# One ring for inputs and attention outputs, per-unit clock figures, and ScalarE row spreads in a two-layer attention kernel

## Chip, core and metric

The kernel runs on one core of a Trainium2 chip. The metric is the device time of one execution in microseconds (us): the median of three runs, 1835.46 us, with the lowest at 1834.81 and the highest at 1835.81.

## What is computed

Two independent attention layers, A and B, each with an input x of 2048 x 1024, a projection `wqkv` (1024 x 3072), 32 heads of size 32, and an output projection `wo` (1024 x 1024), all in float32. Their outputs are set side by side.

```python
qkv = (x @ wqkv).reshape(B, S, 3, 32, 32)            # q, k, v of each head
# A: each position looks at itself and 7 earlier ones, two apart
idx  = pos[:, None] - (arange(8) * 2)[None, :]       # masked where idx < 0
# B: each position looks at the last 256
mask = (i - j >= 0) & (i - j < 256)
out  = softmax(q k^T * 32**-0.5, masked) @ v         # per head
y    = out.reshape(B, S, 1024) @ wo
concatenate([a, b], axis=-1)
```

## The kernel before

**Units.** The work is cut into eight units of 512 positions: four of layer B ("dense" units, 0 to 3), then four of layer A ("window" units, 4 to 7). Each unit has eight head groups s = 0 to 7 of four heads. For a group the kernel computes q and k (`qk_items`, matmul at L526); values come in three parts of four, two and two groups (`v_items`, L591); the output projection of a unit (`o_items`, L652) runs within the next unit. A float32 product is made of three matmuls on a high and a low part of each operand.

**Splits.** Weights and x arrive by DMA in raw tiles. `Stream.parts` makes the high part by a cast, on ScalarE (L203) or VectorE (L206), and the low part by a subtraction on VectorE (L209). Items are split in one order. x tiles come from a pool of 9, the outputs of attention (`finish`: high part by ScalarE, L838, low part by VectorE, L842) from another of 10.

**Dense heads.** The first pass multiplies keys and queries (L873); VectorE masks and finds the maximum (L878); ScalarE exponentiates in place and sums (L883). From maximum and logarithm of the sum comes one number a row, as high and low part (L901 to L904). A small matmul turns the numbers into rows (L912). The row spread writes them below the 96 rows of the queries, VectorE in four instructions, one for each head (L918); keys have ones there, so that the second pass (L956) gives logarithms of the weights at once. ScalarE exponentiates them (L963), GpSimd or VectorE zeroes what is masked (L942, L945), and L1003 multiplies with the values.

**Window heads.** Scores at L722, softmax on VectorE and ScalarE (L730 to L758), a transpose (L761), and a placement of its pieces by ScalarE, eight pairs of copies a head (L770, L773). L788 multiplies with the values.

**The order of the work.** Nothing is reordered on the chip. When the program is built, a planner with a clock of its own (class `Clock`) keeps the expected time at which each engine is free. In turn it takes, from four lists (row matmuls, second passes, first passes, projections), the entry that can start first, writes it out for TensorE, and charges prices such as these:

```python
if ck.ends("act", n / 1200 + 0.06, t0) <= ck.ends("dve", n / 1932 + 0.08, t0) + bias:
e = ck.use("dve", 0.61, ck.now)          # one row spread
```

An engine waits on semaphores for real inputs, so an entry that the planner set too early makes TensorE wait. `MASK_BIAS`, `KEYS_LATE`, `ROWS_LATE`, `SEAT_LATE`, `EDGE_LATE` and `BANK_LATE` are allowances in this clock. `ASK` says after which of an item's eight steps the next weights are split. `V_SLOTS` and `O_SLOTS` say after or before which group's q and k a value part or an output projection stands.

**Unit edges.** The last value part of a unit (16 projection steps) holds the split of the next unit's x, at its steps 1, 5, 9 and 13 (`XAT`). Since items are split in order, the first of these brings the second half of the value weights and the next unit's first q weights with it.

Of the kernel before, what the change touches and what calls it, by code (L numbers as in the profile page):

```python
# [32 lines left out]
V_SLOTS = {0:0,5:1,7:2}  # L33
O_SLOTS = {2: (0, 1), 3: (2, 3), 4: (4, 5), 5: (6, 7)}
V0_SLOTS = {1:0,3:1,7:2}
NX, NST, NN = 9, 1, 3
TAIL, XAT = 4, 1
# [3 lines left out]
BANK_LATE = 0.0  # L41
# [91 lines left out]
class Stream:  # L133
# [3 lines left out]
    def __init__(self, nc, ck, raws, wpool, xpool, items, more, light):  # L137

        self.nc, self.ck, self.raws, self.wpool, self.xpool, self.more = nc, ck, raws, wpool, xpool, more
        self.items = items  # L140
        self.raw, self.tiles, self.ready = {}, {}, {}
        self.loaded = self.split = 0
        self.light = light
        self.load_to(NRAW + len(more))
# [20 lines left out]
    def split_to(self, n):  # L165
        while not self.split:
# [3 lines left out]
            for h in range(2):  # L170
                c = slice(h * S, h * S + S)
                self.tiles[0].append(self.xpool.tile([P, 2, S], F32R, tag="x", name="x"))
                self.ready[0].append(self.parts(self.tiles[0][h], rx[:, c], tx[h], True))
                self.ready[1].append(self.parts(w[:, :, c], rw[:, c], tw[h], True))
# [3 lines left out]
        while self.split < min(n, len(self.items)):  # L178
# [3 lines left out]
            if self.items[i][0] != "w":  # L182
                self.tiles[i], self.ready[i] = [], []
                for h in range(2):
                    t = self.xpool.tile([P, 2, S], F32R, tag="x", name="x")
# [10 lines left out]

    def parts(self, t, raw, t0, side):
# [3 lines left out]
        bias = EARLY if side else LIGHT if self.split >= self.light else SIDE_W if n > S else SIDE_X  # L201
        if ck.ends("act", n / 1200 + 0.06, t0) <= ck.ends("dve", n / 1932 + 0.08, t0) + bias:
            nc.scalar.copy(t[:, 0, :], raw)  # L203
            r = ck.use("act", n / 1200 + 0.06, t0)
        else:
            nc.vector.tensor_copy(t[:, 0, :], raw)  # L206
            r = ck.use("dve", n / 1932 + 0.08, t0)
# [5 lines left out]
    def ahead(self, i, two):  # L213

        for n in range(i + 1, min(i + (3 if two else 2), len(self.items))):
            if self.items[n][0] == "x":
                break
            self.split_to(n + 1)
# [7 lines left out]
def kernel(ctx, tc, xs, wqk, wv, wo, outs, units):  # L226
# [11 lines left out]
    pickp = ctx.enter_context(tc.tile_pool(name="pickp", bufs=1))  # L238
    opool = ctx.enter_context(tc.tile_pool(name="opool", bufs=NO))
# [11 lines left out]

    plan = []
    for u in range(U):
        for s in range(NG):
            if u and s in O_SLOTS:
                plan += [("o", u - 1, n) for n in O_SLOTS[s]]
            plan.append(("qk", u, s))
            vs = V_SLOTS if u else V0_SLOTS
# [7 lines left out]
    def item(key, kind, ap):  # L266
        where[key] = len(items)
        items.append((kind, ap))

    def unit_x(u, *gs):  # L270
        for g in gs or range(4):
            item(("x", u, g), "x", xs[u][:, 2 * g:2 * g + 2, :])

# [5 lines left out]
    for p in plan:  # L279
# [3 lines left out]
        elif p[0] == "v":  # L283
            s0, n = VPARTS[p[2]]
# [6 lines left out]
        elif p[0] == "qk":  # L291
            for t in range(2):
                if p + (t,) not in where:
                    item(p + (t,), "w", wqk[ly, 2 * p[2] + t])
        else:
            if NG - 1 in V_SLOTS:
                item(("qk", p[1], 0, 0), "w", wqk[units[p[1]][0], 0])
                unit_x(p[1])
            else:
                unit_x(p[1], 0)  # L300
                item(("qk", p[1], 0, 0), "w", wqk[units[p[1]][0], 0])
                unit_x(p[1], 1, 2, 3)
# [3 lines left out]
                where[("qk",) + LIGHT_FROM + (0,)] if LIGHT_FROM[0] < U else len(items))  # L306
# [6 lines left out]
    def constants():  # L313
# [13 lines left out]
        pick = cst["pick"] = pickp.tile([32, 16], F32, name="pick")  # L327
        nc.gpsimd.memset(pick, 0.0)
        for row in (0, 16):
            nc.gpsimd.affine_select(pick, pick, pattern=[[-1, 16]], compare_op=ALU.not_equal, fill=1.0, base=-row,  # L330
                                    channel_multiplier=1)
# [14 lines left out]
        def ones():  # L346
            zero = cst["mask_d"][96:P, None, P:2 * P].to_broadcast([32, 24, P])
            for t in kst:
                nc.scalar.activation(t[96:P, :, :].rearrange("p j (a s) -> p (j a) s", s=P), zero, AF.Identity,
                                     bias=1.0, scale=1.0)  # L350
                ck.use("act", 2.7, ck.now)
# [4 lines left out]
    vbuf = [const.tile([P, 6, n * P], F32, name=f"vbuf{i}") for i, (_, n) in enumerate(VPARTS)]  # L356
    vpart = {s0 + i: (p, i * P) for p, (s0, n) in enumerate(VPARTS) for i in range(n)}
# [46 lines left out]
    def qk_items(u, s):  # L404
# [36 lines left out]
        def by_head(c0, c1, e):  # L441

            def go():
# [4 lines left out]
                if c0:  # L448
                    done["nat"][nat] = e2
                    done["stack"][u, s] = e2 + (EDGE_LATE if s == NG - 1 and u + 1 < U else SEAT_LATE)  # L450
# [7 lines left out]
        def evac(t, ps, bank):  # L458
# [7 lines left out]
            def low():  # L466
# [5 lines left out]
                def stack():  # L472
                    e2 = place(1, e)
                    if t == 1:
                        done["stack"][u, s] = max(e2, h2["hi"]) + KEYS_LATE
# [29 lines left out]
        for t in range(2):  # L505
# [15 lines left out]
            def run(k, t=t, h=h):  # L521
# [6 lines left out]
                if k == ASK:  # L528
                    st.ahead(where["qk", u, s, t], not dense and TWO)
# [22 lines left out]
    def v_items(u, part):  # L552
# [5 lines left out]
        s0, ng = VPARTS[part]  # L558
# [47 lines left out]
        def ahead(i):  # L606
            st.ahead(i - 1, TWO and not units[u][2] and not wide)

        def after(r, n, k, b):
            if n == len(rounds[r]) - 1 and k == kw - 1:  # L610
                per = 1 if wide else 2
                c = (4 * u + (2 * r + b if wide else 2 * b)) % 6
                t = copy_out(vbuf[part][:, c:c + per, :], h[b][0].rearrange("p (a f) -> p a f", a=per), h[b][1], rg)
# [15 lines left out]
    def o_items(u, n):  # L629
# [15 lines left out]
        def run(k):  # L645
# [8 lines left out]
            if k == ASK and (not last or n == 0 or n > 2):  # L654
                if last:
                    st.split_to(where["o", u, n] + (3 if n == 0 else 2))
                else:
                    st.ahead(where["o", u, n], TWO and u + 1 < U and not units[u + 1][2])
# [32 lines left out]
    def window(u, s):  # L691
# [5 lines left out]
        vp, vc = vpart[s]  # L697
        v = vbuf[vp]
# [53 lines left out]
        def total(e):  # L752
# [7 lines left out]
            for i in range(2):  # L760
                nc.vector.transpose(turned[i], band[buf][:, 768 * i:768 * i + 768])  # L761
                e = ck.use("dve", 1.02, ck.now)
                ck.defer(e - 0.1, lambda i=i, e=e: spread(i, e))

        def spread(half, e):
            pieces = turned[half].rearrange("p (j b t c) -> p j b t c", j=2, b=4, t=3)
            diag = wide[buf][:, 2 * half:2 * half + 2].rearrange("p j (b c) -> p j b c", b=4)
            for i in range(4):
                r, c = 32 * i, 32 * i + 8
                nc.scalar.copy(diag[r:r + 32, :, :, c:c + 32], pieces[r:r + 32, :, :, 1 + i % 2, :])  # L770
                ck.use("act", 0.34, e)
                n, c = ((i - 1) * 32, c) if i else (96, 0)
                nc.scalar.copy(diag[n:n + 32, :, :, c:c + 8], pieces[r:r + 32, :, :, i % 2, :8])  # L773
                t = ck.use("act", 0.21, e)
            if half:
                h["p"] = t

        def values_ready():
            if hg >= NO and ((hg - NO) // NG, NG - 1) not in done["out"]:
# [70 lines left out]
    def attention(u, s):  # L850
# [6 lines left out]
        vp, vc = vpart[s]  # L857
        v = vbuf[vp]
# [35 lines left out]
        def log_sum():  # L894
# [4 lines left out]
            def parts():  # L899
# [5 lines left out]
                e2 = ck.use("dve", 0.52, e, port=True)  # L905
                aux.append(Item(lambda: latest(rs.when(BANK_LATE), e2), lambda: rows(hl), 0.08))

            ck.defer(e, parts)

        def rows(hl):  # L910
# [3 lines left out]
            def spread():  # L914

                h["rows"] = []
                for j in range(4):
                    nc.vector.tensor_tensor(q[96:P, j, :].rearrange("p (b s) -> p b s", s=P),  # L918
                                            ps[0:32, None, 0:P].to_broadcast([32, 4, P]),
                                            cst["pick"][0:32, 4 * j:4 * j + 4, None].to_broadcast([32, 4, P]), op=ALU.mult)  # L920
                    e = ck.use("dve", 0.61, ck.now)
                    h["rows"].append(e + ROWS_LATE)
# [4 lines left out]
        for b in range(4):  # L927
            for j in range(4):
                one.append(Item(lambda: latest(rs.when(BANK_LATE), done["stack"].get((u, s))),
# [9 lines left out]
        def keep(w, mask, n, m, step, base, chan, r):  # L939
            dur_p, dur_d = m * n / 960 + 0.13, m * n / 960 + 0.07  # L940
            if ck.ends("pool", dur_p, r) <= ck.ends("dve", dur_d, r, port=True) + MASK_BIAS:
# [39 lines left out]
        def second_ready(ki, hp):  # L981
# [4 lines left out]
            return latest(rs.when(BANK_LATE), h["rows"] and h["rows"][hp * pack + pack - 1])  # L986

        def values_ready(ks):
            if ks[-1] == nk - 1 and hg >= NO and ((hg - NO) // NG, NG - 1) not in done["out"]:
# [27 lines left out]
        for i, ks in enumerate(lots):  # L1017
            for ki in ks:
                pack = kbs[ki][3]
                for hp in range(4 // pack):  # L1020
# [3 lines left out]
                            C3 + sum(kbs[k][2] / 592 for k in ks)))  # L1024
# [9 lines left out]
    xt[0], xready[0] = [], []  # L1034
    for p in plan:
# [111 lines left out]
```

## Time and profile before

| quantity | value |
|---|---|
| median of three runs | 1835.46 us |
| the profiled execution | 1834.72 us |
| its span | 1832.6 us |
| TensorE matmul busy | 1805.0 us |
| weight loads busy | 1468.2 us |
| VectorE / ScalarE / GpSimd busy | 1300.5 / 966.2 / 395.3 us |
| mean granted TensorE clock | 0.996 |

A row of the waits says which line on which engine stood still, who ended that, how long in total, how often, and the longest. A row of the timeline has start, length, engine, line, operation, tiles and count; in square brackets is the idle time before it. A row of stages has the stage, its length, the busy time and count of TensorE, weight loads, VectorE, ScalarE and GpSimd, the granted clock, the share of the DMA engines and GB/s.

### The profile page before, as it was taken

The numbers are of one execution on the slowest core, as the hardware profiler recorded it, in microseconds if no ns is written. First come the engines' busy times: TensorE is split into PE (matmuls) and PEld (weight loads), VectorE is DVE, ScalarE is ACT, GpSimd is POOL, SyncE is SP. The second block draws the span as 40 slices with busy tenths as digits, with TensorE's granted clock in tenths as the row PEclk, the third lists the DMA queues.
The fourth block names the chain that finished last, engine by engine and source line by source line (L and its number), as shares of the span: only waits on it lengthen the run. The fifth ranks groups of instructions, "written<-read, shape, count | busy, mean of one in ns | idle before, by whom it ended". The sixth has DMA issues, their size and how long they took to land.

```text
span 1832.6 us, 34542 instructions
## 1 busy us (share of the span) xinstructions
PE 1805.0 (98%) x12778; PEld 1468.2 (80%) x12778; DVE 1300.5 (71%) x2718; ACT 966.2 (53%) x2520; POOL 395.3 (22%) x920
## 2 busy tenths in 40 slices
PE   9999999999999999999999999999999999999999
PEld 7787787888778788788887688878887788778887
DVE  6677886768867679776687486776667667766773
ACT  5566566565655555656555364544445444534452
POOL 2322313232242324232223200110011100110000
PEclk9999999999999999999999999999999999999999
DMA  7445665545555556545444333343434443434332
GB/s 242 125 134 139 177 169 144 170 121 166 160 154 163 152 146 174 141 149 144 135 136 139 106 126 128 127 133 127 136 120 133 138 132 107 156 122 138 123 104 81
DMA packets 109128, 257.20 MB, mean 140 GB/s; under 512 B 14496, under 2 KB 29856, under 8 KB 108960
## 3 DMA queue, kind: packets, MB, share of 16 engines
q0 software_dynamic: 41760, 152.06, 26.7%
q1 hardware_dynamic: 56832, 83.00, 17.0%
q10 hardware_dynamic: 10368, 19.93, 2.9%
q8 instruction: 101, 1.65, 0.4%
q14 instruction: 67, 0.55, 0.1%
HBM read 164.63 MB, written 23.07 MB: 102 GB/s over the span
## 4 chain that ended last, share of the span: by engine, by line
PE 90%; ACT 5%; DVE 3%; issue 1%; DMA 1%; POOL 0%; ACTq 0%; POOLq 0%; DVEq 0%
PE g L526 36%; PE g L652 19%; PE g L591 16%; PE s L956 5%; PE s L873 5%; PE o L1003 5%; PE o L788 2%; ACT wide L770 2%; PE s L722 1%; ACT wide L773 1%; DVE band L758 1%; DVE sm L754 1%; DVE w L209 1%; DMA raw<-xs 1%; ACT s L883 0%
## 5 line engine op out<-in xcount | busy, mean ns | idle before, releaser
L526 PE MATMUL g<-x,w 128*128 128x512 f32 x3072 | 774.9, 395 | 3.7 <-DVE w L206 1.7
L526 PEld LDWEIGHTS g<-x,w 128*128 128x128 f32 x3072 | 565.9, 189 | 118.0 <-issue 5.8
L591 PE MATMUL g<-w,x 128*128 128x256 f32 (+1 forms) x2304 | 389.3, 320 | 2.0 <-DVE w L209 2.0
L209 DVE TENSOR_TENSOR w<-raw,w 128x512 fp32r<-128x512 f32 x516 | 337.5, 696 | 34.7 <-ACT w L203 27.7
L591 PEld LDWEIGHTS g<-w,x 128*128 128x128 f32 x2304 | 332.5, 190 | 30.6 <-DVE w L209 3.6
L652 PE MATMUL g<-ot,w 128*128 128x512 f32 x1416 | 345.4, 395 | 1.1 <-ACT ot L838 0.7
L883 ACT ACTIVATE s<-s,nm 128x384 f32<-128x384 f32 (+2 forms) x512 | 274.3, 536 | 112.3 <-DVE nm L878 112.1
L878 DVE CUSTOM_DVE_ANT_0 s<-s,mask_d 128x384 f32<-128x384 f32 (+2 forms) x512 | 261.5, 553 | 84.6 <-PE s L873 83.9
L652 PEld LDWEIGHTS g<-ot,w 128*128 128x128 f32 x1416 | 264.7, 189 | 57.2 <-ACT ot L838 1.6
L942 POOL TENSOR_SCALAR_AFFINE_SELECT pbuf<-pbuf 128x128 f32<-128x128 f32 (+1 forms) x604 | 220.2, 393 | 323.8 <-ACT pbuf L963 322.4
L963 ACT ACTIVATE pbuf<-s 128x384 f32<-128x384 f32 (+2 forms) x480 | 202.6, 505 | 68.1 <-PE s L956 66.5
L206 DVE CAST w<-raw 128x1024 fp32r<-128x1024 f32 x188 | 132.5, 705 | 70.4 <-PE g L652 26.0
L161 POOL DMA_DIRECT2D raw<-wqk x126 | 68.5, 543 | 425.6 <-DVE w L209 303.4
L956 PEld LDWEIGHTS s<-qst,kst 128*128 128x128 f32 x704 | 113.1, 188 | 42.0 <-ACT s L883 17.3
L873 PE MATMUL s<-kst,qst 96*128 96x384 f32 (+2 forms) x512 | 141.9, 341 | 0.9 <-ACT s L883 0.7
L956 PE MATMUL s<-qst,kst 128*128 128x256 f32 (+2 forms) x704 | 137.1, 302 | 4.1 <-ACT s L883 3.0
L770 ACT COPY wide<-wide 32x256 f32<-32x256 f32 x256 | 103.3, 404 | 58.0 <-DVE wide L761 55.0
L873 PEld LDWEIGHTS s<-kst,qst 96*128 96x128 f32 x512 | 93.3, 189 | 25.5 <-issue 4.1
L544 ACT COPY ost<-g 128x512 f32<-128x512 f32 x51 | 29.9, 587 | 157.8 <-PE g L652 157.8
L161 POOL DMA_DIRECT2D raw<-wo x64 | 34.5, 540 | 331.1 <-DVE w L209 210.2
L883 ACT ACTIVATION_READ_ACCUMULATOR s<-s,nm 128x1 f32 x512 | 105.3, 206 | 0.0
L842 DVE TENSOR_TENSOR ot<-o,ot 128x512 fp32r<-128x512 f32 x64 | 43.9, 686 | 80.9 <-ACT ot L838 80.9
(77 smaller groups left out, 1395.4 us busy)
## 6 DMA issues: line engine op xcount, KB each, us to landing
raw<-wqk POOLq DMA_DIRECT2D x126, 512.0 KB, 3.8
raw<-wv POOLq DMA_DIRECT2D x72, 512.0 KB, 4.2
raw<-wo POOLq DMA_DIRECT2D x64, 512.0 KB, 3.8
qst<-nat SPq DMA_DIRECT2D x96, 256.0 KB, 4.9
kst<-nat SPq DMA_DIRECT2D x96, 256.0 KB, 5.5
raw<-xs POOLq DMA_DIRECT2D x28, 512.0 KB, 4.3
outs<-ost ACTq DMA_DIRECT2D x56, 256.0 KB, 2.0
kst<-halo SPq DMA_DIRECT2D x72, 128.0 KB, 4.2
```

The costliest lines, as they stand in the source:

```text
L206: nc.vector.tensor_copy(t[:, 0, :], raw)
L209: nc.vector.tensor_tensor(t[:, 1, c:c + 512], raw[:, c:c + 512], t[:, 0, c:c + 512].bitcast(F32), op=ALU.subtract)
L526: nc.tensor.matmul(h["ps"], h["w"][:, a, k * P:(k + 1) * P], xt[u][k][:, b, :], start=(k == 0 and i == 0), stop=(k == NK - 1 and i == 2))
L591: nc.tensor.matmul(ps, xt[u][kw * g + k][:, a, p0:p0 + P], h["w"][g][:, c, k], start=(first and t == 0 and half == 0), stop=(last and t == 2),
L652: nc.tensor.matmul(h["ps"], w[:, a, c:c + P], ot[u, k][:, b, :], start=(k == 0 and i == 0), stop=(k == NK - 1 and i == 2))
L770: nc.scalar.copy(diag[r:r + 32, :, :, c:c + 32], pieces[r:r + 32, :, :, 1 + i % 2, :])
L873: nc.tensor.matmul(ps[:, :n], q[0:96, j, b * P:(b + 1) * P], kk[0:96, j, c0:c1], start=True, stop=True)
L878: nc.vector.tensor_tensor_reduce(ps[:, :n], ps[:, :n], mask[:, cut:full], scale=-1.0, scalar=BIG, op0=ALU.add, op1=ALU.min, accum_out=nm)
L883: nc.scalar.activation(ps[:, :n], ps[:, :n], AF.Exp, bias=nm, scale=-1.0, accum_out=sm)
L942: nc.gpsimd.affine_select(w, w, pattern=[[0, m], [step, n]], compare_op=ALU.is_ge, fill=0.0, base=base, channel_multiplier=chan)
L956: nc.tensor.matmul(ps[:, i * n:(i + 1) * n], kk[:, j, 256 + kb * P:256 + (kb + 1) * P], q[:, j, q0:q0 + n], start=True, stop=True)
L963: nc.scalar.activation(w, ps[:, :pack * n].rearrange("p (j n) -> p j n", j=pack), AF.Exp)
```

## The change

- The pools of 9 and 10 tiles become one ring of 19. Its tiles are taken in the order of use; a value step of attention is held back when the tile that comes next belongs to attention outputs whose projection isn't done.
- Tables `EDGES_V` tell before which of the 32 steps of a unit's last q, k and value items each item is split: the last k weights (k7), the two value weights (v0, v1), the next q weights (q0), the four x items. `EDGE_AT` picks one of four tables for each unit. The tables `EDGES_K`, `VPARTS_LATER` and the lags are for value layouts that no unit uses.
- The allowances become a tuple for each unit (`PACE`): for dense units mask bias, lateness of keys, rows and banks, an extra price of the value step, split bias, ask; for window units lateness of seats and edge, split bias, lateness of the pieces, how many items are split ahead, ask.
- Prices: split casts n/1200 + 0.1 and n/1932 + 0.19; the three small steps 0.58; transpose 0.88; the pieces 0.415 and 0.255.
- The row spread moves to ScalarE, one instruction for each block of 128 queries and all four heads. The ones below the keys become, for each head, ones in that head's rows alone, made by eight ScalarE copies in place of two. The table `pick` is 32 x 4, and `heads` is new; both are made by GpSimd with 16 selects where there were 2.
- Unit 5's second value part goes one group later; unit 6 takes its output projections one group earlier; unit 7's last two go one group later.

```diff
-NRAW, NP, NO, NS = 3, 768, 10, 4
-ASK = 2
+NRAW, NP, NS = 3, 768, 4
-SIDE_X, SIDE_W = -99, -99
-TWO = True
-LIGHT, LIGHT_FROM = 0.5, (4, 1)
-MASK_BIAS = 0.2
-ROWS_LATE, KEYS_LATE = 0, 1.2
-SEAT_LATE = 4.0
-EDGE_LATE = 7.0
-NX, NST, NN = 9, 1, 3
-TAIL, XAT = 4, 1
+NX, NST, NN = 19, 1, 3
+PACE = ((0.1, 1.2, 0.1, 0.0, 0.0, -99, 2), (0.2, 1.2, 0.0, 0.0, 0.2, -99, 1), (0.2, 1.2, 0.0, 0.0, 0.0, -99, 2), (0.2, 0.6, 0.0, 0.0, 0.2, -99, 2), (4.0, 7.0, 0.5, 0.0, 1, 2), (4.0, 7.0, 1.5, 0.5, 1, 1), (4.0, 7.0, 0.5, 0.2, 1, 3), (4.0, 7.0, 0.5, 0.0, 1, 2))
+EDGE_AT = (0, 3, 0, 1, 0, 0, 2, 0)
+EDGES_V = (
+    ((2, "k7"), (10, "v0"), (17, "v1"), (17, "q0"), (17, "x0"), (21, "x1"), (25, "x2"), (29, "x3")),
+    ((2, "k7"), (6, "x0"), (10, "v0"), (18, "v1"), (19, "x1"), (23, "x2"), (26, "q0"), (27, "x3")),
+    ((2, "k7"), (10, "v0"), (14, "x0"), (18, "v1"), (20, "x1"), (24, "x2"), (26, "q0"), (28, "x3")),
+    ((2, "k7"), (10, "v0"), (16, "x0"), (18, "v1"), (19, "q0"), (20, "x1"), (24, "x2"), (28, "x3")))
...
+    def tile(self, what):
+        self.ring.append(what)
+        return self.xpool.tile([P, 2, S], F32R, tag="x", name="x" if what is None else "ot")
+
+    def next_holds(self):
+
+        return self.ring[len(self.ring) - NX] if len(self.ring) >= NX else None
...
-        if ck.ends("act", n / 1200 + 0.06, t0) <= ck.ends("dve", n / 1932 + 0.08, t0) + bias:
+        if ck.ends("act", n / 1200 + 0.1, t0) <= ck.ends("dve", n / 1932 + 0.19, t0) + bias:
...
-            zero = cst["mask_d"][96:P, None, P:2 * P].to_broadcast([32, 24, P])
+            zero = cst["mask_d"][96:P, None, P:2 * P].to_broadcast([32, 6, P])
             for t in kst:
-                nc.scalar.activation(t[96:P, :, :].rearrange("p j (a s) -> p (j a) s", s=P), zero, AF.Identity,
-                                     bias=1.0, scale=1.0)
-                ck.use("act", 2.7, ck.now)
+                for j in range(4):
+                    nc.scalar.activation(t[96:P, j, :].rearrange("p (a s) -> p a s", s=P), zero, AF.Identity,
+                                         bias=cst["heads"][96:P, j:j + 1], scale=1.0)
+                    ck.use("act", 0.73, ck.now)
...
-                ck.use("act", 0.34, e)
+                ck.use("act", 0.415, e)
...
-                t = ck.use("act", 0.21, e)
+                t = ck.use("act", 0.255, e)
...
-        o = opool.tile([P, 2, S], F32R, tag="ot", name="ot")
+        o = st.tile(u)
...
-                h["rows"] = []
-                for j in range(4):
-                    nc.vector.tensor_tensor(q[96:P, j, :].rearrange("p (b s) -> p b s", s=P),
-                                            ps[0:32, None, 0:P].to_broadcast([32, 4, P]),
-                                            cst["pick"][0:32, 4 * j:4 * j + 4, None].to_broadcast([32, 4, P]), op=ALU.mult)
-                    e = ck.use("dve", 0.61, ck.now)
-                    h["rows"].append(e + ROWS_LATE)
+                for b in range(4):
+                    nc.scalar.activation(q[96:P, :, b * P:(b + 1) * P], ps[0:32, None, 0:P].to_broadcast([32, 4, P]),
+                                         AF.Copy, scale=cst["pick"][0:32, b:b + 1])
+                    e = ck.use("act", 0.485, ck.now)
+                h["rows"] = e + PACE[u][2]
                 rs.give(bank, e)
...
-            return latest(rs.when(BANK_LATE), h["rows"] and h["rows"][hp * pack + pack - 1])
+            return latest(rs.when(PACE[u][3]), h["rows"])
```

More of the change, by code (lines that the diff above doesn't have):

```diff
@@ L143, in __init__ @@
         self.light = light
+        self.ring = []
         self.load_to(NRAW + len(more))
@@ L211, in parts, with ahead @@
         return end
[L213 to L218, printed above, removed]
+    def ahead(self, i, two=False):
+        left = 2 if two else 1
+        for n in range(i + 1, len(self.items)):
+            if self.split <= n and (self.items[n][0] == "x" or self.items[n][2]):
+                return
+            if self.items[n][0] != "x":
+                self.split_to(n + 1)
+                left -= 1
+                if not left:
+                    return
     def get(self, i):
@@ L292 @@
             for t in range(2):
-                if p + (t,) not in where:
+                if p + (t,) not in where and not (p[2] == NG - 1 and t and p[1] + 1 < U and NG - 1 in slots_of(p[1])):
                     item(p + (t,), "w", wqk[ly, 2 * p[2] + t])
         else:
[L296 to L302, printed above, removed]
+            u = p[1] - 1
+            for at, key in edge_of(u):
+                if key[0] == "x":
+                    unit_x(u + 1, key[2])
+                elif key[0] == "qk":
+                    item(key, "w", wqk[units[key[1]][0], 2 * key[2] + key[3]], True)
+                else:
+                    item(key, "w", wv[units[u][0], parts_of(u)[key[2]][0] + key[3]], True)
+    light = [0.0] * len(items)
+    for key, i in where.items():
+        u = min(key[1] + (key[0] == "o"), U - 1)
+        light[i] = PACE[u][5] if units[u][2] else PACE[u][2]
     pbuf = const.tile([P, 4, NP], F32, name="pbuf")
@@ L326, in constants @@
                                 channel_multiplier=1)
[L327 to L331, printed above, removed]
+        pick = cst["pick"] = const.tile([32, 4], F32, name="pick")
+        heads = cst["heads"] = const.tile([P, 4], F32, name="heads")
+        for t, step, rows in ((pick, -1, [4 * i for i in range(8)]),
+                              (heads[96:P], -4, [i + r for r in (0, 16) for i in range(4)])):
+            nc.gpsimd.memset(t, 0.0)
+            for row in rows:
+                nc.gpsimd.affine_select(t, t, pattern=[[step, 4]], compare_op=ALU.not_equal, fill=1.0, base=-row,
+                                        channel_multiplier=1)
         cst["mask_d"] = bands("mask_d", 384, 0.0, FAR, (1, -1, -1), (-1, 256, 1))
@@ L606, in ahead @@
         def ahead(i):
-            st.ahead(i - 1, TWO and not units[u][2] and not wide)
+            st.ahead(i - 1, not units[u][2] and not wide and PACE[u][4])
         def after(r, n, k, b):
@@ L657, in run @@
                 else:
-                    st.ahead(where["o", u, n], TWO and u + 1 < U and not units[u + 1][2])
+                    st.ahead(where["o", u, n], u + 1 < U and not units[u + 1][2] and PACE[u + 1][4])
             if k == 5 and last and n in (1, 2):
```

124 lines of the change are left out of this document (77 added, 47 removed), and 4 rows, old and new, of the table EDGES_K.

## The prediction, made before the result was known

> **What bounds the kernel.** I read the page first, then TensorE's waits, then matmul spacing, stages and single steps.
>
> ```profile
> span 1832.6 us, 34542 instructions
> ...
> PE 1805.0 (98%) x12778; PEld 1468.2 (80%) x12778; DVE 1300.5 (71%) x2718; ACT 966.2 (53%) x2520; POOL 395.3 (22%) x920
> ...
> L526 PE MATMUL g<-x,w 128*128 128x512 f32 x3072 | 774.9, 395 | 3.7 <-DVE w L206 1.7
> ```
>
> TensorE is the bound over the whole span: 1832.6 less 1805.0 leaves 27.6 us in which it shows nothing. The diff leaves every matmul count alone, so only idle time, and idle time that hides inside "busy", can move. How much hides there is told by the spacing:
>
> ```profile
> 1057.50 4.70 PE L652 MATMUL g<-ot,w 128*128 128x512 f32 x20
> ```
>
> Twenty matmuls took 4.70 us. Less one mean length (0.395), 4.305 over 19 steps is 0.227 us a matmul. A matmul is drawn 0.395 long while its successor may start after 0.227, so any stall loses 0.17 us more than the profile calls idle. The visible idle has these reasons:
>
> ```profile
> engine line waited for: us in total, times, longest us
> PE o L788 <- ACT wide L773: 5.3, 8, 1.0
> PE s L956 <- ACT s L883: 3.0, 4, 1.1
> PE o L1003 <- POOL pbuf L942: 2.7, 1, 2.7
> PE s L912 <- DVE hl L904: 2.6, 3, 2.0
> PE g L591 <- DVE w L209: 2.0, 3, 1.6
> PE g L526 <- DVE w L206: 1.7, 2, 0.9
> PE s L1071 <- DVE qst L1068: 1.5, 1, 1.5
> PE g L526 <- ACT x L203: 1.1, 1, 1.1
> ...
> PE g L526 <- ACT w L203: 0.6, 1, 0.6
> ```
>
> These nine are 20.5 us. No wait is for a DMA, for an x tile held too long, or for the row spread. Each is a place where the order written out by the planner put a matmul a little before its input was there. The order is fixed when the program is built, so a wrong price in the planner's clock becomes a wait, and TensorE does not turn to other work. That makes the clock figures the part of the change to cost first. Three stretches matter besides:
>
> ```profile
> 440.00:470.00 30.00, 29.03 (x187) 23.00 (x186) 27.87 (x69) 15.36 (x42) 10.67 (x21) 1.00 0.71 202
> ```
> ```profile
> 1035.00:1042.00 7.00, 6.84 (x17) 5.12 (x18) 2.68 (x4) 0.69 (x2) 0.55 (x1) 0.55 0.49 162
> 1586.00:1596.00 10.00, 8.26 (x53) 5.67 (x52) 7.92 (x13) 8.57 (x19) 0.88 (x2) 0.83 0.25 82
> ```
>
> Around the edge from unit 1 to 2 VectorE is busy 27.87 of 30 us and ScalarE 15.36: there VectorE is nearly a second bound. After the last dense head, and again near 1590, the granted clock falls to 0.55 and 0.83.
>
> **Clock figures (about -8.1).** First the piecewise copies that lay out a window head's weights:
>
> ```profile
> 1395.47 0.41 ACT L770 COPY wide<-wide 32x256 f32<-32x256 f32 x1 [2.47 <-DVE wide L761]
> 1395.89 0.24 ACT L773 COPY wide<-wide 32x64 f32<-32x64 f32 x1
> 1396.15 0.40 ACT L770 COPY wide<-wide 32x256 f32<-32x256 f32 x1
> ```
>
> From start to start they take 0.42 and 0.26. The old planner prices 0.34 and 0.21, and eight pairs a head make it early by 8 x (0.68 - 0.55) = 1.04 us. That is the longest wait of L788 (1.0). The new prices, 0.415 and 0.255, leave 0.08. Where the planner knows, it runs projection matmuls instead, so of 5.3 us I take away 4.8. Next the split casts:
>
> ```profile
> 20.24 0.68 DVE L206 CAST w<-raw 128x1024 fp32r<-128x1024 f32 x1
> 20.96 1.29 DVE L209 TENSOR_TENSOR w<-raw,w 128x512 fp32r<-128x512 f32 x2
> ```
> ```profile
> 1391.01 1.99 ACT L203 CAST w<-raw 128x1024 fp32r<-128x1024 f32 x2
> ```
>
> VectorE's step is 0.72. The old price is 1024/1932 + 0.08 = 0.61, the new one 0.72. ScalarE's two in 1.99 bound a step between 0.95 and 1.0 (old 0.91, new 0.95). The waits that end on w splits are 2.0 + 1.7 + 0.6 = 4.3 us. The largest, 1.6, is longer than one cast's error of 0.11 explains, so I take half, 2.3. Last the three little steps ahead of the row matmul:
>
> ```profile
> 177.68 0.18 DVE L901 TENSOR_TENSOR nl<-nm,ln 128x16 f32<-128x16 f32 x1 [0.69 <-ACT ln L896]
> 177.89 0.17 DVE L903 CAST hl<-nl 128x16 fp32r<-128x16 f32 x1
> 178.10 0.17 DVE L904 TENSOR_TENSOR hl<-nl,hl 128x16 fp32r<-128x16 f32 x1
> ```
>
> They take 178.27 - 177.68 = 0.59, priced 0.52 before and 0.58 after. That mends two short waits; the 2.0 us one began earlier, so of 2.6 I take 1.0. Bounds for the whole item: nothing, if the waits only change place, and all 12.2 us.
>
> **Rows on ScalarE (about +1.0).** Removed from VectorE, four a head:
>
> ```profile
> L918 DVE TENSOR_TENSOR qst<-s,pick 32x512 fp32r<-32x512 f32 x128 | 79.3, 676 | 10.0 <-PE s L912 9.4
> ```
>
> That frees 79.3 us of VectorE in the dense units. Nobody on TensorE waits for these rows now, so the gain is indirect, where VectorE is full: three dense edges at some 0.7 us, -2.0 (bounds 0 and -4, the second being most of what waits on VectorE outside the items above). Added is a ScalarE copy from PSUM with a per-partition scale, which the trace does not have. Nearest are these:
>
> ```profile
> L463 ACT ACTIVATE nat<-g 128x512 fp32r<-128x512 f32 x64 | 38.3, 598 | 93.8 <-PE g L526 83.3 <-DMA qst<-nat 7.0 <-DMA halo<-nat 2.9
> L883 ACT ACTIVATE s<-s,nm 128x384 f32<-128x384 f32 x448 | 249.1, 557 | 95.3 <-DVE nm L878 95.1
> ```
> ```profile
> 491.90 0.54 ACT L883 ACTIVATE s<-s,nm 128x384 f32<-128x384 f32 x1
> 492.36 0.20 ACT L883 ACTIVATION_READ_ACCUMULATOR s<-s,nm 128x1 f32 x1
> ```
>
> The second has a per-partition operand. Its successor starts 0.46 after it. With 128 more elements at 1/1200 us, 0.107, the step is 0.567, and four end 2.37 us after the first began, with a tail of 0.1. The planner prices 4 x 0.485 = 1.94 and adds 0.15 until an end is seen, so it is early by 0.28; at the first row's price (0.598 less the same overlap) by nothing. The edit also makes all second-pass matmuls wait for all four rows, not two:
>
> ```profile
> 178.68 2.48 DVE L918 TENSOR_TENSOR qst<-s,pick 32x512 fp32r<-32x512 f32 x4 [0.40 <-PE s L912]
> 179.96 0.34 PE L956 MATMUL s<-qst,kst 128*128 128x384 f32 x1
> ```
>
> Here the second pass began 1.28 us after the first row, right after two of them. The planner knows of that wait and puts projection matmuls there, so it costs nothing while they last. The 0.28 is felt where the second pass is set at once. Between 0 and 32 x 0.28 = 9 us I take a third, +3.0. Queued behind the four rows on ScalarE are the exponentials that free the score banks; ScalarE's 53% covers that on the mean.
>
> The Trainium skill speaks against this move. "ScalarE: Activation LUTs", Rules for kernel authors, gives multiplications to VectorE, and its section What ACT_TABLE_LOAD costs has 186 ns plus 0.833 ns an element, some 93 more for a pointer operand and 93 of overlap. By that a row copy is an estimated 0.61 us a step and my +3.0 would be about +4.8. The trace's pointer row (557) lies below the 600 that the page gives for 384 elements.
>
> **Edges (-1.5).** Table 0 repeats the old places: x at 17, 21, 25 and 29, with v1 and q0 forced ahead of x0. So four of seven edges do not change. From unit 1 to 2 things move by one or two items, from 3 to 4 and 6 to 7 x0 goes 11 and 3 items earlier and q0 nine later. This spreads VectorE's burst. I allow 0.5 us each, between +1 and -2 each.
>
> **Ring, seats in the plan, start (0).** 9 + 10 tiles become 19. No wait above is for either, so the ring only makes table 1's early x0 possible. A value step held back for its tile is covered by projection work. The moved o and v slots, asks and lateness of single units I put at 0, within 3 either way. At the start:
>
> ```profile
> 1.49 0.45 POOL L330 TENSOR_SCALAR_AFFINE_SELECT pick<-pick 32x16 f32<-32x16 f32 x2
> 8.25 1.23 POOL L161 DMA_DIRECT2D raw<-wqk x2 [0.16 <-issue]
> ```
> ```profile
> 22.34 5.42 ACT L349 ACTIVATE kst<-mask_d 32x3072 fp32r<-32x3072 f32 x2
> ```
>
> GpSimd gets 14 more selects and a memset, at up to 0.22 us some 3.3, and its first loads go out near 11.6. They are first read by the cast at 20.24, so the cover is some 8 us less their flight; without it the 3.3 would show whole. The ones become eight ScalarE copies of 768 elements, 0.74 by the pointer row, 5.9 us against 5.42. Projections hide it.
>
> **Hidden time (-2.2).** Some eight stalls gone take 0.17 each with them, 1.4 in all. A clock of 0.83 over the ten us near 1590 loses at most 1.7; two stalls of the kinds above lie there, and I take half, 0.8. The 0.55 stretch stays, since what comes before it is GpSimd's mask (the 2.7 us wait).
>
> **Sum.** -8.1 + 1.0 - 1.5 + 0 - 2.2 = -10.8. The profiled execution took 1834.72 us (span 1832.6 and 2.1 around it), 0.74 below the median of 1835.46. So 1823.9 for it, 1824.7 for the median.
>
> **Rivals.** *Order pays everything (0.16).* All visible waits but the start's 2.6 go (18 of these rows), with 0.17 for some 20 of them (3.4) and both cold stretches, 0.45 x 7 = 3.2 and 0.8. That is -25, with rows' +1.0 near 1811; 1806 to 1816. For it speaks that every wait is a planner's error, against it that one price per kind cannot fit all. [...]
>
> *Waits are dealt anew (0.14).* Another order has other ties; what L788 gives back appears as waits for ScalarE's casts and exponentials. Gain and loss cancel: 1831.8 to 1839.
>
> *ScalarE becomes the wait (0.12), slower.* Rows stand ahead of exponentials in one queue, and four score banks wait on these. If TensorE stands 0.28 for the rows and another 0.4 for a bank in each of 32 heads, that is 22 us, 19 more than counted: about 1844. It decides the sign from (10.8 + 3.0)/32 = 0.43 us a head. For it: the 3.0 us that L956 already waits on L883. Against it: only four waits in 32 heads.
>
> **How the numbers follow.** The forecast case has 0.58 and runs from 1816 to 1831. Faster means over 0.2% (3.7 us, about what a measurement of this kernel can tell from no change): 0.58 + 0.16 = 0.74. The redealt case gives 0.12 to the same and 0.02 to slower, which with ScalarE's 0.12 is 0.14. The range, 1810 to 1839, leaves out most of the slower rival and the lower end of the first.
>
> **What would show it.** Right: L788's wait on L773 under 1 us in all; no VectorE row spread, 128 ScalarE copies of 0.6 to 0.7 us in its place, VectorE's busy time near 1221 and ScalarE's near 1040; TensorE idle near 18 us; a clock of 1.00 near 1590. Wrong: a wait of L956 for the rows' line over 8 us in all, longer waits for L883, or new waits as large as the ones gone.

## The result, and the profile after

The changed kernel takes 1806.05 us (median of four runs, 1805.01 to 1807.37) against 1835.63 for the kernel before beside it: a ratio of 0.9836, with a 95% interval of 0.9819 to 0.9853. It is faster by 29.6 us. The forecast was 1824.7, and its range ended at 1810.

The page of the changed kernel (first the span, then busy time, share and count by engine):

```profile
span 1803.3 us, 34584 instructions
...
PE 1788.7 (99%) x12778; PEld 1462.7 (81%) x12778; DVE 1229.5 (68%) x2631; ACT 1036.7 (57%) x2643; POOL 386.9 (21%) x905
```

The same 12778 matmuls run. Idle time of TensorE is 1803.3 - 1788.7 = 14.6 us, down from 27.6: 13.0 of the 29.3 that the span lost. The mean granted clock went from 0.996 to 1.0. The execution before has three stretches with a granted clock of 0.50 (3.4 us from 10.5, 6.8 from 1034.5, 3.4 from 1590.9); these 13.6 us cost at most half their length, 6.8 us, and the changed one has none of them (its other runs have mean clocks of 0.998 to 1.0, so one or two such stretches come and go by chance). By subtraction the remaining 9.5 us were lost in stalls that a matmul's drawn length hides; no row shows them.

TensorE's waits after:

```profile
PE s L923 <- DMA kst<-nat: 1.8, 2, 1.1
PE s L1134 <- DVE qst L1131: 1.5, 1, 1.5
PE g L576 <- ACT x L216: 1.3, 1, 1.3
PE g L641 <- DVE w L222: 1.2, 3, 0.7
PE s L962 <- DVE hl L954: 1.2, 1, 1.2
PE s L1005 <- ACT qst L968: 1.0, 2, 0.7
```

The 5.3 us for the pieces of the window heads are gone, and so is the 2.7 for GpSimd's mask. What waits are left are short, the longest 1.5 us at the start. From 1167 us to the end only one wait of 0.7 us is left.

Where in the kernel the time went is told by q and k matmuls, 384 a unit. These are the stages of the kernel before, cut where a unit's first one starts (length; busy time and count of this line alone), from unit 3 on:

```profile
699.97:955.97 256.00, 102.40 (x384) 69.84 (x385) 1.00 0.53 148
955.97:1180.85 224.88, 91.96 (x384) 71.08 (x385) 0.98 0.40 126
1180.85:1380.75 199.90, 91.64 (x384) 70.99 (x385) 1.00 0.40 131
1380.75:1580.55 199.80, 91.36 (x384) 71.08 (x385) 1.00 0.40 129
1580.55:1829.10 248.55, 92.59 (x384) 71.65 (x384) 0.99 0.36 116
```

And of the changed kernel:

```profile
697.50:956.50 259.00, 101.53 (x384) 70.35 (x384) 1.00 0.54 152
956.50:1167.70 211.20, 91.69 (x384) 71.27 (x384) 1.00 0.39 126
1167.70:1362.80 195.10, 89.87 (x384) 71.41 (x384) 1.00 0.40 130
1362.80:1558.20 195.40, 89.84 (x384) 71.49 (x384) 1.00 0.41 133
1558.20:1799.70 241.50, 90.10 (x384) 71.46 (x384) 1.00 0.36 122
```

The dense units end where they ended (956.0 and 956.6). Unit 4 gained 13.7 us, units 5 to 7 with the tail 4.8, 4.4 and 7.0. Two numbers sum this up: the start of unit 5 (1180.9 before, 1167.8 after) and the time from there to the last matmul (648.2 and 631.9).

The change in unit 4 can be watched. The kernel before, at the end of its last dense head:

```profile
1026.25 2.67 PE L956 MATMUL s<-qst,kst 128*128 128x384 f32 x12
1028.85 1.43 PE L1003 MATMUL o<-pbuf,vbuf 128*32 128x384 f32 x8
1032.98 1.49 PE L1003 MATMUL o<-pbuf,vbuf 128*32 128x256 f32 x16 [2.70 <-POOL pbuf L942]
1035.16 9.44 PE L652 MATMUL g<-ot,w 128*128 128x512 f32 x27 [0.69 <-ACT ot L838]
```

There were no projections left: the next, L652, needs the output of this very head. TensorE waited for the masks, waited for the output, and then ran 27 matmuls in 9.44 us, where 27 x 0.227 is 6.1. The wait and this slow stretch are 2.7 and 3.3 us of the 13.7 that unit 4 gained; the rest is not seen in single rows. The changed kernel at the same place:

```profile
1013.87 0.97 PE L1005 MATMUL s<-qst,kst 128*128 128x384 f32 x4
1014.68 0.84 PE L576 MATMUL g<-x,w 128*128 128x512 f32 x3
...
1017.61 3.63 PE L702 MATMUL g<-ot,w 128*128 128x512 f32 x15
1021.17 2.31 PE L1052 MATMUL o<-pbuf,vbuf 128*32 128x384 f32 x24
1024.16 0.50 PE L702 MATMUL g<-ot,w 128*128 128x512 f32 x1 [0.69 <-ACT ot L888]
1024.89 6.19 PE L702 MATMUL g<-ot,w 128*128 128x512 f32 x26 [0.22 <-DVE ot L892]
```

The last part of the head's second pass starts at 1013.87 instead of 1026.25, and projections (L576, L702) stand among it. The long wait and the slow clock are gone.

### The profile page after: what moved, and what is told of

Same layout as the page of the kernel before. It is cut to its first block, busy times and chain, and to the rows that moved or that the text cites. A ratio compares the mean times of both kernels' runs of the same rounds, so it can differ in the third digit from the quotient of the medians.

```text
span 1803.3 us, 34584 instructions
## 1 busy us (share of the span) xinstructions
PE 1788.7 (99%) x12778; PEld 1462.7 (81%) x12778; DVE 1229.5 (68%) x2631; ACT 1036.7 (57%) x2643; POOL 386.9 (21%) x905
## 3 DMA queue, kind: packets, MB, share of 16 engines
q0 software_dynamic: 41760, 152.06, 26.6%
## 4 chain that ended last, share of the span: by engine, by line
PE 94%; DMA 2%; ACT 2%; DVE 2%; issue 0%; POOL 0%; ACTq 0%; SPq 0%; DVEq 0%
PE g L576 38%; PE g L702 19%; PE g L641 18%; PE s L1005 6%; PE s L923 5%; PE o L1052 5%; PE o L838 2%; PE s L772 1%; DMA kst<-nat 1%; DMA halo<-nat 1%; ACT qst L968 1%; DVE s L928 0%; DVE w L222 0%; DMA raw<-xs 0%; ACT kst L391 0%; DMA qst<-nat 0%
## 5 line engine op out<-in xcount | busy, mean ns | idle before, releaser
L576 PE MATMUL g<-x,w 128*128 128x512 f32 x3072 | 763.7, 393 | 2.4 <-ACT x L216 1.3
L576 PEld LDWEIGHTS g<-x,w 128*128 128x128 f32 x3072 | 567.1, 188 | 111.5 <-issue 3.2
L702 PE MATMUL g<-ot,w 128*128 128x512 f32 x1416 | 344.0, 393 | 0.9 <-ACT ot L888 0.7
L702 PEld LDWEIGHTS g<-ot,w 128*128 128x128 f32 x1416 | 261.8, 188 | 56.1 <-issue 1.8
L991 POOL TENSOR_SCALAR_AFFINE_SELECT pbuf<-pbuf 128x128 f32<-128x128 f32 (+1 forms) x574 | 205.9, 386 | 267.7 <-ACT pbuf L1012 263.7
L1005 PEld LDWEIGHTS s<-qst,kst 128*128 128x128 f32 x704 | 108.9, 189 | 36.0 <-ACT s L933 13.2
L1005 PE MATMUL s<-qst,kst 128*128 128x256 f32 (+2 forms) x704 | 132.1, 303 | 1.4 <-ACT qst L968 1.0
L166 POOL DMA_DIRECT2D raw<-wv x72 | 46.4, 644 | 279.7 <-DVE w L222 167.9
L594 ACT COPY ost<-g 128x512 f32<-128x512 f32 x44 | 25.8, 586 | 120.2 <-PE g L702 120.2
```

The lines of the kernel that those rows point to most:

```text
L166: (self.nc.scalar if early else self.nc.gpsimd).dma_start(raw if len(ap.shape) == 2 else raw.rearrange("p (a b) -> p a b", a=2), ap)
L576: nc.tensor.matmul(h["ps"], h["w"][:, a, k * P:(k + 1) * P], xt[u][k][:, b, :], start=(k == 0 and i == 0), stop=(k == NK - 1 and i == 2))
L702: nc.tensor.matmul(h["ps"], w[:, a, c:c + P], ot[u, k][:, b, :], start=(k == 0 and i == 0), stop=(k == NK - 1 and i == 2))
L991: nc.gpsimd.affine_select(w, w, pattern=[[0, m], [step, n]], compare_op=ALU.is_ge, fill=0.0, base=base, channel_multiplier=chan)
L1005: nc.tensor.matmul(ps[:, i * n:(i + 1) * n], kk[:, j, 256 + kb * P:256 + (kb + 1) * P], q[:, j, q0:q0 + n], start=True, stop=True)
```

## The experiments

Two theories were set against each other. *Prices*: wrong prices made the waits, so each right price gains its own share wherever it is put. *Fitting*: the order is one solution of many figures chosen together, so a part alone gains nothing and any part taken back spoils it. In the table "from unit 5" is the time from unit 5's first q matmul to the last matmul; both stage columns are of the profiled execution, the median and ratio of all runs beside the kernel before.

| kernel | median us | ratio to before (95%) | unit 5 starts | from unit 5 |
|---|---|---|---|---|
| before | 1835 | 1 | 1180.9 | 648.2 |
| changed | 1806.05 | 0.9836 (0.9819, 0.9853) | 1167.8 | 631.9 |
| 1 before, piece prices | 1843.00 | 1.0042 (1.0027, 1.0057) | 1183.9 | 653.6 |
| 2 before, cast prices | 1844.07 | 1.0051 (1.0036, 1.0066) | 1188.2 | 651.9 |
| 3 before, rows on ScalarE | 1841.10 | 1.0034 (1.0022, 1.0047) | 1186.5 | 652.5 |
| 4 before, all three | 1851.93 | 1.0094 (1.0079, 1.0109) | 1191.9 | 652.9 |
| 5 changed, old piece prices | 1824.91 | 0.9943 (0.9927, 0.9959) | 1171.5 | 647.5 |
| 6 changed, one set of allowances | 1819.93 | 0.9916 (0.9898, 0.9934) | 1178.6 | 636.3 |
| 7 changed, old slots | 1815.53 | 0.9897 (0.9879, 0.9916) | 1169.6 | 639.3 |
| 8 changed, table 0 everywhere | 1818.90 | 0.9915 (0.9900, 0.9929) | 1177.7 | 635.8 |
| 9 changed, rows on VectorE | 1832.68 | 0.9988 (0.9977, 0.9999) | 1195.8 | 632.1 |
| 10 changed, neutral figure | 1807.63 | 0.9848 (0.9829, 0.9867) | 1171.4 | 631.8 |
| 11 before, neutral figure | 1833.68 | 0.9992 (0.9982, 1.0001) | 1179.9 | 646.6 |
| 12 before, ring | 1834.77 | 1.0000 (0.9991, 1.0010) | 1182.3 | 646.1 |
| 13 changed, old cast prices | 1811.49 | 0.9868 (0.9852, 0.9885) | 1174.1 | 631.9 |
| 14 changed, table 0 at edge 3 to 4 | 1814.99 | 0.9885 (0.9870, 0.9899) | 1176.5 | 632.4 |
| 15 changed, table 0, two pools | 1828.49 | 0.9958 (0.9943, 0.9973) | 1178.3 | 644.5 |
| 16 before, window part | 1836.01 | 1.0003 (0.9994, 1.0013) | 1181.4 | 647.4 |
| 17 as 3, old addresses | 1834.92 | 0.9996 (0.9986, 1.0005) | 1183.1 | 647.1 |
| 18 as 15, old addresses | 1821.07 | 0.9923 (0.9908, 0.9938) | 1176.2 | 640.1 |

**Parts alone on the kernel before (1 to 4).**

```diff
 1: -ck.use("act", 0.34, e)      +ck.use("act", 0.415, e)
    -t = ck.use("act", 0.21, e)  +t = ck.use("act", 0.255, e)
    -e = ck.use("dve", 1.02, ck.now)  +e = ck.use("dve", 0.88, ck.now)
 2: -n / 1200 + 0.06, n / 1932 + 0.08  +n / 1200 + 0.1, n / 1932 + 0.19
    -e2 = ck.use("dve", 0.52, e, port=True)  +e2 = ck.use("dve", 0.58, e, port=True)
 3: the row spread, the ones, pick and heads as in the change, lateness 0
 4: 1 + 2 + 3
```

> The kernel before with only the three prices of window heads changed (pieces 0.415 and 0.255, transpose 0.88). If right prices mend waits wherever they stand (theory of prices), the 5.3 us of waits of the window values for the pieces fall under 1 us, units 4 to 7 get shorter by 8 to 12 us with the hidden part and the slow clock near 1590, and the time is 1823 to 1828. If each order just deals waits anew and only figures fitted to one order gain (theory of fitting), the time stays within 4 us of 1835.6, with other waits in their place. The dense units, to 956 us, keep their times under both.

> The kernel before with only the prices of the split casts and of the three small steps changed. Theory of prices: the waits for w splits (4.3 us) halve and those for the row numbers (2.6 us) shrink by 1; 1829 to 1833, with changes in all units. Theory of fitting: within 4 us of 1835.6 either way.

> The kernel before with only the row spread moved to ScalarE (and the ones and tables that it needs), lateness 0. If the move helps by freeing VectorE at the dense edges, 1831 to 1834; if it costs what the prediction put on it (+3 for late rows, -2 for VectorE), 1836 to 1837; if ScalarE becomes the wait, 1840 or more. In the trace of the whole change the dense units ended at 956.6 against 956.0, so no effect within 3 us is the likeliest.

> The kernel before with all new prices and the row spread on ScalarE, but with its own pools, edges, slots and one set of allowances. Theory of prices: most of the gain, 1812 to 1822. Theory of fitting: little of it, 1828 to 1838, and the rest lies in the figures of single units, the slots and the edge tables.

All four are slower, and 1, 2 and 4 are slower than either theory had said; 3 reached its third range, though not for the reason given there, as 17 shows. The theory of prices fell in this form: with the right price of the pieces the wait that it was to mend did not shrink. The first run's row:

```profile
PE o L788 <- ACT wide L773: 6.9, 7, 2.3
```

It was 5.3 in 8. The 16 copies took 5.38 us as now priced (from 1188.27 to 1193.65 in one head), but they began late, behind VectorE's transpose. What the planner had wrong ahead of that was not traced: with the cast prices alone (number 2) this wait is 12.5 us in 10, and with all prices right (number 4) still 4.7 in 7. Kernels 3 and 4 hold an artifact besides, which 17 shows.

**Parts taken out of the changed kernel (5 to 8).**

```diff
 5: the three prices of 1 put back
 6: -PACE = ((0.1, 1.2, 0.1, ...
    +PACE = ((0.2, 1.2, 0.0, 0.0, 0.0, -99, 2),) * 4 + ((4.0, 7.0, 0.5, 0.0, 1, 2),) * 4
 7: V_AT and O_AT of units 5 to 7 as in units 1 to 4
 8: -EDGE_AT = (0, 3, 0, 1, 0, 0, 2, 0)
    +EDGE_AT = (0,) * 8
```

> The changed kernel with only the three old prices of window heads put back (pieces 0.34 and 0.21, transpose 1.02). The first four runs say that no price alone gains anything on the kernel before. Theory of fitting (all figures were chosen together for one order, so any one of them moved spoils it): 1815 to 1830, with waits of the window values for the pieces of 3 us or more. Rival (the gain lies in the ring, slots and allowances, which leave slack whatever the prices): 1806 to 1811.

> The changed kernel with one set of allowances for all dense units and one for all window units, as before the change (mask bias 0.2, keys 1.2, nothing else; seats 4, edge 7, bias 0.5, no lateness of pieces, ask 2). Theory of fitting: 1818 to 1835. Rival (ring and slots carry the gain): 1806 to 1812.

> The changed kernel with the value parts and output projections of units 5, 6 and 7 at their old places. The units after 4 gained 4.8, 4.4 and 7.0 us of 29. Theory of fitting: 1812 to 1825, with most of the loss after 1160 us. If the places themselves give the gain, the loss is at most these 16 us and lies in units 5 to 7 alone; if they do nothing, 1805 to 1807.

> The changed kernel with the old places of the splits at every edge (table 0). The dense units ended at 956.6 against 956.0 before, so edges 1 to 2 and 3 to 4 can hardly have gained by themselves; by the prediction the tables are worth 1.5. Theory of fitting: 1811 to 1825 all the same, since every later time shifts. Rival (tables matter little): 1805 to 1809.

Each costs 9 to 19 us, within what fitting expected, and mostly in its own stage. Number 7 does not decide, since its loss lies within its rival's bound of 16 us too. The pieces' prices cost 15.6 of their 18.9 us from unit 5 on, which is nearly all that these units had gained. The fifth run's waits:

```profile
PE g L576 <- DVE w L222: 5.9, 3, 3.3
PE o L838 <- ACT wide L823: 3.7, 6, 1.0
```

The slots cost 7.4 there, the edge table 9.9 before unit 5 and 3.9 after (the edge from 6 to 7), one set of allowances 10.8 and 4.4.

**Rows, controls, ring (9 to 12).**

```diff
  9: the row spread, ones and pick of the kernel before, in the changed kernel
 10, 11: -    SEM = 0.2  +    SEM = 0.205
 12: one ring of 19 and its hold rule in the kernel before, nothing else
```

> The changed kernel with the row spread back on VectorE (the old ones and table, lateness 0, each second pass released by its own heads' rows). On the kernel before, the move cost 5.7 us. Theory of fitting: the move is worth nothing by itself, but the figures of units 0 to 3 were chosen with it, so 1812 to 1826 with the loss before 960 us. Rival (the move itself frees VectorE in the dense units): the same sign, but with waits of TensorE on VectorE in the dense units (splits, row numbers) of 3 us or more above those of the changed kernel.

> A control: the changed kernel with the planner's allowance for a semaphore at 0.205 instead of 0.2 us, five nanoseconds that are no better or worse as a description of the chip. Theory of fitting: the order changes in many places and the time rises by 5 to 15 us, to 1811 to 1821. Theory of prices and places: within 3 us of 1806.

> The same control on the kernel before. Theory of fitting: the kernel before was a fitted order as well, so 1838 to 1847, as much as the right prices cost it in the first three runs. If the kernel before was an ordinary order, the time falls or rises alike, within 4 us of 1835.

> The kernel before with only the two pools joined to one ring of 19. No wait of the kernel before was for a tile, so the prediction put the ring at 0: 1833 to 1838. If VectorE's splits at the edges were held up by tiles that TensorE still read, which the waits of TensorE alone do not show, 1825 to 1832.

The neutral figure puts another kind of matmul into 753 of the 12778 places of the changed kernel's order and costs 1.6 us there, with intervals that overlap. In the kernel before it does so in only 18 places, so that control says little; its 1.1 us of gain can't be told from nothing. So fitting in its strong form, that any other order is worse, fell: five nanoseconds do not matter, a tenth of a microsecond in the right place does. The ring alone is worth nothing.

The rows on VectorE cost 26.6 us, all ahead of unit 5, though the same move alone gave the kernel before nothing (17). The ninth run's waits:

```profile
PE s L958 <- DVE hl L950: 8.9, 5, 2.9
PE o L1049 <- POOL pbuf L988: 2.7, 1, 2.7
```

VectorE comes late with the row numbers five times (8.9 us; 1.2 in the changed kernel), the dense units end at 973.2 (16.6 us later), and behind them the wait for GpSimd is back: the last dense head again stands without projections. The time lies above the range of fitting, and the sign that its rival named came: the move frees VectorE. How much of the 26.6 us is that relief, and how much the allowances of units 0 to 3, which were set beside the moved rows, was not separated.

**What was still open (13 to 16).**

```diff
 13: the cast prices and the 0.58 of the small steps put back in the changed kernel
 14: -EDGE_AT = (0, 3, 0, 1, 0, 0, 2, 0)  +EDGE_AT = (0, 3, 0, 0, 0, 0, 2, 0)
 15: 8, and pools of 9 and 10 tiles with the old hold rule in place of the ring
 16: the kernel before, with piece prices and lateness, and from unit 4 on cast prices,
     split bias, asks and slots as in the change
```

> The changed kernel with only the prices of the split casts and of the three small steps put back. If they are needed because the rest was fitted with them, 1812 to 1825; if they only cost time, as on the kernel before (12 us in the dense units), 1796 to 1804. Stage by stage: the end of the dense units (956.6) and the window units 5 to 7 (632) tell where.

> The changed kernel with table 0 at the edge from unit 3 to 4 alone. If early x at that edge lets the last dense head start its second pass while projections are left, this one entry brings back the 2.7 us wait for GpSimd, the half clock near 1030 and 10 us: 1814 to 1819. If the three changed edges act together, 1806 to 1812.

> The changed kernel with table 0 at every edge and the two old pools of 9 and 10 tiles, to be set against the run with table 0 at every edge and the ring (1818.9). If the ring does nothing beside making other tables possible, 1816 to 1822; if it also takes waits of the splits away, 1823 or more.

> The kernel before with the window part of the change: prices of pieces and transposes, cast prices and split bias from unit 4 on, lateness of the pieces 0.5 and 0.2 in units 5 and 6, slots and asks of units 5 to 7; old pools, old edges, rows on VectorE. If the parts of the change act by stages, units 5 to 7 take 632 to 638 us instead of 648 and the time is 1818 to 1826. If the window figures work only behind the new dense units and edges, 1830 to 1840.

Number 14 hits: one entry of one table is 8.9 us. The dense units end 4.3 us earlier (952.3), unit 4 takes 224.2 us instead of 211.2, and the old picture returns:

```profile
1028.86 1.85 PE L1052 MATMUL o<-pbuf,vbuf 128*32 128x256 f32 x16 [2.70 <-POOL pbuf L991]
1031.40 2.80 PE L702 MATMUL g<-ot,w 128*128 128x512 f32 x5 [0.69 <-ACT ot L888]
```

Here five matmuls take 2.80 us, at half speed (the granted clock from 1030 to 1038 us is 0.68). The reading that fits, not traced step by step, is that the table slows the projections a little ahead of the edge, and so keeps some for the last head.

The other kernels bear out what the wait costs. Nine have this wait of 2.7 us (before, 1, 2, 8, 9, 11, 12, 14, 16). In each a half-speed stretch of 3.4 or 6.8 us begins within 2 us of the wait's end, and unit 4 takes 219.8 to 226.4 us. The other eleven do not have the wait, nor that stretch behind the last dense head, and unit 4 takes 209.7 to 219.4. The table alone does not decide it: 15 and 18 have table 0 and not the wait, 9 has the new tables and the wait.

Number 13 missed both its numbers by little: old cast prices cost 5.4 us in the changed kernel, all ahead of unit 5, and nothing from there on. Number 15 reached its second range, 1823 or more, as if the ring took waits away; 18 shows another reason.

Number 16 fell into its second range: the window part alone leaves units 5 to 7 at 647.4. Its waits:

```profile
PE g L596 <- DVE w L214: 4.5, 4, 2.2
PE g L657 <- DVE w L214: 3.3, 1, 3.3
...
PE o L793 <- ACT wide L778: 2.0, 3, 1.6
```

The pieces' wait fell from 5.3 to 2.0 us, and waits for weight splits grew in its place (2.0 for the values before; now 4.5 for the values and 3.3 for the output projections). Here the prices did what they say, and the gain was dealt out again.

**The same kernels at old addresses (17, 18).** Kernels 3 and 15 had something else in common. Near the end of each kernel stands an unbroken row of 96 output projection matmuls: before, number 3, and number 17.

```profile
1807.15 21.92 PE L652 MATMUL g<-ot,x 128*128 128x512 f32 x96
```
```profile
1816.47 22.56 PE L656 MATMUL g<-ot,x 128*128 128x512 f32 x96
```
```profile
1808.26 21.92 PE L656 MATMUL g<-ot,x 128*128 128x512 f32 x96
```

Less the last one's drawn length of 0.39, 95 steps take 227 ns, 233 and 227. In number 3 nearly all output projections have the slow step: of the 1435 that follow one another the median is 233 ns, against 227 before and in 17, and 1435 x 6 ns is 8.6 us. No other kind of matmul changed its median step by more than 1 ns, and in all kernels but 3, 4 and 15 such a row of 96 takes 21.92 us, in 9 too, so that its loss is no matter of addresses. The order of TensorE's matmuls in 3 and 17 is the same. The edit changes only where two small tables lie: in 3 they take 32 bytes of the pool of constants, in 17 a 64-byte tile ahead of the pool of attention outputs, where the old table was.

```diff
-pick = cst["pick"] = const.tile([32, 4], F32, name="pick")
-heads = cst["heads"] = const.tile([P, 4], F32, name="heads")
+both = pickp.tile([P, 16], F32, name="pick")
+pick, heads = cst["pick"], cst["heads"] = both[:32, :4], both[:, 4:8]
```

> The kernel before with the row spread on ScalarE, as in the third run, but with both small tables in a 64-byte tile where the old one was, so that every later tile has its old address; TensorE's order is the third run's, instruction for instruction. If the place makes the 6 ns, the output projections step at 227 ns again and the time falls by 7.7 us to 1832 to 1835. If the row spread itself slows them (ScalarE's reads or writes beside them), it stays at 1840 to 1843.

> The changed kernel with table 0 and two pools, as in the fifteenth run, with the 64 bytes put back ahead of the pool of attention outputs. If the place makes the 6 ns and the ring does nothing else, 1818 to 1823 beside 1818.9 with the ring; if the ring takes waits away, 1826 or more.

Both hit. So the loss of 5.7 us in number 3 is the address, and so are, by the same step, some 6 to 9 of number 4's 16.6 us. The move of the rows alone is worth nothing on the kernel before (0.9996), but only as a sum: in 17 the dense units end at 968.5 instead of 956.0, and unit 4, without the wait for GpSimd, takes 214.6 us instead of 224.9. The ring against two pools is 1818.9 against 1821.07, with intervals that overlap: not told from nothing.

## Why the prediction was wrong

The bound, the direction, and the reason, that the waits come from the planner's figures, held. The size did not: -10.8 forecast, -29.6 measured. Nearly all signs named for the forecast came (no wait for the pieces, 128 copies of 0.665 us, VectorE at 1229.5 us and ScalarE at 1036.7, a clock of 1.00 near 1590), so they could not tell it from the rival. The rival *order pays everything*, given 0.16, said 1806 to 1816, some -24; it comes nearest, with both cold stretches and about half of the visible idle time gone. That 1806.05 lies just inside its range is partly luck: it took 18 us of visible idle away, where 13.0 went, and 7.4 us of hidden time, where 16.3 went.

The step that failed is the sum itself: one term for each edit, each taking its own waits and leaving the rest alone. Runs 1 to 4, 12 and 16 show that none of the parts tried alone gains anything on the kernel before. Runs 5 to 9 and 13 show that each of six parts is worth 5 to 27 us once the others are there. These six losses add up to 87 us, three times the gain, so no table of shares exists. By its own terms the sum missed most in the last one: it took 8.6 us of visible idle away (-8.1 + 1.0 - 1.5), where 13.0 went, and 2.2 of hidden time, where 16.3 went. Of the 18.5 us that it missed of the span, 14.1 are hidden time, sized by eight visible stalls and 0.8 us of clock.

Term by term:

- **Clock figures, -8.1.** The steps read from the trace were right, as was the end of L838's waits. Alone they cost 7.6 and 8.7 us; in the changed kernel the pieces' prices are worth 18.9 and the cast prices with the small steps 5.4. Working from the rows of waits could give neither number.
- **Rows, +1.0.** The row copy was sized well. In the changed kernel:

```profile
L968 ACT ACTIVATE qst<-s,pick 32x512 fp32r<-32x512 f32 x128 | 76.3, 665 | 20.8 <-PE s L962 20.4
```
```profile
178.36 2.39 ACT L968 ACTIVATE qst<-s,pick 32x512 fp32r<-32x512 f32 x4
```

  Four take 2.39 us (forecast 2.37), a step of 0.575. TensorE waits 1.0 us for them in two places, not 3.0. The failing part is the other one: VectorE's relief was put at -2.0 with a bound of -4, and putting the rows back costs 26.6 us in company. The rule of the Trainium skill ("ScalarE: Activation LUTs", Rules for kernel authors) that gives multiplications to VectorE would have kept the rows there; the ninth run shows 1832.68 for that. The estimate of 0.61 us a step from its section What ACT_TABLE_LOAD costs lies above the 0.575 here.
- **Edges, -1.5.** Edge 3 to 4 alone is 8.9. The failing sentence is that the 0.55 stretch stays, since GpSimd's mask comes before it. TensorE stands for the mask only where nothing else is left to run; run 14 brings wait and slow clock back together by moving splits of weights and x.
- **Slots and allowances, 0 within 3.** 9.5 and 13.9 by runs 7 and 6.
- **Ring, 0.** Runs 12 and 18 show no effect that can be told from nothing. **Start.** Nearly: the ones took 6.70 us instead of 5.9 (a step of 0.46 and 384 more elements at 1/1200 us make 0.78 each, not 0.74) and stood ahead of a key evacuation; TensorE then waited 1.1 us for those keys at 29.5, put at nothing in the prediction.
- **Hidden time, -2.2.** 16.3 us beyond the visible idle, of which up to 6.8 is clock, the 0.55 stretch with it. The rest lay, by subtraction, in stalls that show no idle time to count; where they were is open.

What stays open is which difference between number 16 and the changed kernel's window units carries the rest of their 16 us. The edge table gives 3.9 (run 8). The ring may give some: with table 0 these units take 635.8 us with the ring and 640.1 with two pools (8 and 18), though the whole times hardly differ. The remaining differences are the rule by which the next split is chosen, and the times at which the dense units hand over. They were not separated.

## What to carry to other kernels

When the order of work is fixed ahead by a planner, judge a set of figures as a whole and by stage: its gain is not the sum of its waits, and a right price put alone into a fitted order can cost time. Look first for the places where the filler work runs out, since one wait there can bring a second and a slow clock behind it. And before an edit is blamed for a small loss, compare the step of untouched matmuls, in case it moved their operands in memory.

## What was not expected of the hardware

- Where the tiles of the moving operand lie in memory, shifted by some tens of bytes, changes the step of a 128x512 matmul from 227 to 233 ns (96 matmuls in 21.92 and 22.56 us), 6 to 9 us over this kernel. Which addresses are the good ones was not worked out.
- In this kernel a single wait of 2.7 us was enough to bring a half-speed stretch, in nine kernels of nine: before, the granted clock was 0.55 from 1035 to 1042 us, while TensorE was busy for 4.66 of the 8 us ahead. The changed kernel's profiled execution has a mean clock of 1.0.
- Moving 128 instructions of 0.68 us off an engine that is busy 71% of the span was worth 26.6 us where the rest of the order was set beside it, and nothing on the whole where it was not.
